# The opening of a gated attention and gated FFN kernel: x of the first segment in four tiles, wq by row halves

## The chip, the cores and the metric

The kernel runs on one core of a Trainium2 chip. The metric is device time in microseconds of one execution, as the median of several runs.

## The reference

One input x of 2048 tokens by 512 goes through two branches, and a gate per token mixes them. All tensors are bfloat16.

```python
g = sigmoid((x * gate_w).sum(-1, keepdims=True))
a = _A_ref(x, wq, wk, wv, wo, beta)      # 32 heads of 16, 4 segments of 512 tokens
b = (relu(x @ W_gate) * (x @ W_up)) @ W_down   # F = 1792
out = g * a + (1 - g) * b
```

In `_A_ref` each segment has causal softmax attention of its own (`a_dot`). From the second segment on a memory of the earlier segments is read too: `num = phi(q) @ M`, `den = phi(q) @ z + 1e-6`, with phi(t) = t + 1 for t > 0 and exp(t) otherwise. The two are mixed by a gate per head, sigmoid(beta), and projected by wo. After each segment M and z take in `phi(k)` and v.

## The kernel before

The work is written as some 1350 tasks, each for one engine, with a cost, a priority and what it depends on. Their order is not found when the kernel is built: it is written out by hand as a list of numbers, `ORDER`, and `UNITS` says which of the eight PSUM banks or ring buffers each task takes. So each engine works through a fixed queue. The figures in `LANDS` are the landing times of the first loads that the order was planned with; they make no instruction.

The token axis is cut into four segments of 512 tokens. For each segment TensorE makes q, k and v. The scores of four heads at a time are made in row mode: four matmuls side by side, each on 32 rows of the array. A score group (`score`, `qk`) fills four PSUM banks, ScalarE takes the exp of all four at once, GpSimd masks the diagonal pieces, and TensorE multiplies by v in column mode. Four such fills (`NFILL`) serve one unit of eight heads, and fill f takes heads of parity r = f % 2. Matmuls of the FFN and of the projections fill the time between. A full 128-wide matmul can also be issued as four of 32 columns side by side (lines L476 and L480 are the two forms), which the kernel does where TensorE is in column mode already.

The opening is what the change is about. SP's queue and ACT's queue each issue one DMA of x (`load_x0`, L267: two token tiles of 128 tokens each, the first 256 features) and one chunk of wq (`load_wq`, 128 rows). SP then issues a transposing DMA for the other half of the features (L304), the other two wq chunks, wk, wv and the FFN's weights. Meanwhile TensorE runs seven warm-up matmuls on a constant (`heat`, L922). Then `x0_tasks` turns the x tiles by matmuls with an identity matrix (L513), two token tiles into one bank, and DVE and ACT copy 256 columns at a time into `xT` (L528). ACT's first copy is preceded by its table load. One matmul on zeros, `junk` (L522), stands behind the flips.

`proj_q` of segment 0 takes the four wq chunks one by one, chunk 0 for all four heads' groups first; its results go to `QT` (DVE, L567). `proj_k` writes `ktr` (DVE, L583) and then three tasks write `KT` (L586): the even-parity half by `mcol_e`, the odd half by `mcol_o`, and a piece that only the diagonal groups read. A fill waits for `QT` and all three:

```python
e = score(key, lambda r=r, k=k: qk(u, r, k), [prj["q", seg, c]] + prj["k", seg, c], ...
```

Of the kernel before, what the change touches and what calls it, by code (L numbers as in the profile page):

```python
# [12 lines left out]
P = 128  # L13
# [8 lines left out]
NC = D // P  # L22
# [71 lines left out]
"""  # L94

UNITS = (
    "456701237654305000122212611232212100100000100000000130110000003000300002301130200031220202"
    "14113320353207112630381119110d320b102a221c100102102200031022000121112200033220200104563012"
    "000003200000002201100000320002000020011312212203031113a32230207013430163028200b21350219122"
    "c303d0112011031320210001131302032220322331021456721030000023000000022011000002300020000310"  # L100
    "111220213112163223212b3012121530243008013a01390037612d201c00121201322100312122323022013100"
    "145631200000023000000023011000000000000007001131230220103122362025300b320220081234211a0239"
    "715d4027326c10011200110"
)


class Slot:


    def __init__(self, cands):  # L110
        self.cands, self.units, self.left = tuple(cands), (), 0

    @property
# [66 lines left out]
def kernel(  # L180
# [74 lines left out]
    def work():  # L255
        return plan.one("ps", range(7, -1, -1))


    LANDS = dict(n0=3470, n1=3600, q0=4500, q1=4550, x0=5600, q2=5900, q3=6400, ka=7700,
                 kb=9600, v=11000, g0=12500, u0=13800, gw=14800, be=15100, g1=16300, u1=17500,  # L260
                 n2=18500, x1=21500, g2=22800, u2=23900, g3=25000, u3=26100)

# [726 lines left out]
```

## Time and profile before

| what | us |
| --- | --- |
| median of three runs (263.3 to 263.73) | 263.61 |
| the profiled execution | 263.58 |
| its span on the core | 261.9 |
| TensorE (PE) busy | 254.7 |
| VectorE (DVE) busy | 203.7 |
| ScalarE (ACT) busy | 183.2 |

The span is the time from the first to the last instruction of the core; about 1.7 us of the execution's time lie around it. A line of a timeline gives the start and the busy time of a group of instructions in us, the engine (PEld is the weight load, SPq and ACTq are DMA issues), the line of the kernel, the operation, what is written from what, and how often. In brackets stands how long the engine had been idle and what ended that.

### The profile page before, as it was taken

Reading aid. Unit: us, or ns where it says so; the run is one execution under the profiler, and the core shown is the slowest. Engines: PE = TensorE matmul, PEld = TensorE weight load, DVE = VectorE, ACT = ScalarE, POOL = GpSimd, SP = SyncE. Lnnn points to the kernel's source line nnn. Section 1 sums busy time; section 2 is a strip of 40 time slices with the busy share of each in tenths; the row PEclk is TensorE's granted clock in tenths of the full one; section 3 lists DMA queues with packets and bytes.
Section 4 is the critical chain, followed back from the end, with each engine's and each line's share of the span. In section 5 each row is a group of like instructions: output and inputs, shape, how many; then the busy total and the mean of one; then the engine's idle time right before and its main releaser. Section 6 shows DMA issues by size and latency. Waiting matters only on the chain.

```text
span 261.9 us, 8759 instructions
## 1 busy us (share of the span) xinstructions
PE 254.7 (97%) x3769; PEld 116.9 (45%) x3798; DVE 203.7 (78%) x472; ACT 183.2 (70%) x168; POOL 64.2 (25%) x168
## 2 busy tenths in 40 slices
PE   8899999999999999999999999999999999999995
PEld 3344434453444354544444444445444444445454
DVE  1899999888896756958989868858988678788622
ACT  2199998998877788787768576878486768972100
POOL 8023462313321223222112222122122232120000
PEclk9999999999999999999999999999999999999999
DMA  7999887021411202100210500140200100330011
GB/s 193 293 292 269 221 241 145 4 43 23 84 34 43 92 22 72 45 0 3 83 21 3 95 4 21 55 150 3 80 4 20 32 7 23 97 108 3 3 43 40
DMA packets 31581, 19.71 MB, mean 75 GB/s; under 512 B 16056, under 2 KB 30008, under 8 KB 31544
## 3 DMA queue, kind: packets, MB, share of 16 engines
q1 hardware_dynamic: 31128, 18.90, 27.1%
q8 instruction: 29, 0.48, 0.7%
q10 hardware_dynamic: 416, 0.26, 0.3%
q14 instruction: 8, 0.07, 0.1%
HBM read 13.21 MB, written 2.55 MB: 60 GB/s over the span
## 4 chain that ended last, share of the span: by engine, by line
PE 90%; DVE 5%; issue 1%; DMA 1%; SPq 1%; ACT 0%; DVEq 0%; ACTq 0%
PE ps L476 54%; PE ps L480 19%; PE ps L634 8%; PE ps L707 7%; DMA wq_sb<-in_A_wq_dram 1%; DVE ktr L583 1%; PE ps L647 1%; DVE KT L586 1%; PE ps L827 1%; SPq L304 1%; DVE QT L567 0%; PE ps L763 0%; DVE T L738 0%; DVE hT L877 0%; PE ps L803 0%
## 5 line engine op out<-in xcount | busy, mean ns | idle before, releaser
L656 ACT ACTIVATE E<-ps 128x2048 bf16<-128x2048 f32 x64 | 120.1, 1877 | 32.7 <-PE ps L634 22.5
L685 POOL TENSOR_SCALAR_AFFINE_SELECT E<-E 128x256 bf16<-128x256 bf16 x128 | 55.5, 458 | 170.3 <-ACT E L656 170.3
L877 DVE TENSOR_TENSOR hT<-ps,rgr 128x512 bf16<-128x512 f32 x56 | 37.8, 683 | 13.1 <-PE ps L476 8.4
L476 PE MATMUL ps<-xT,wu_sb 128*128 128x512 bf16 x163 | 45.6, 380 | 0.7 <-issue 0.5
L871 ACT ACTIVATE rgr<-ps 128x512 bf16<-128x512 f32 x56 | 32.6, 596 | 15.3 <-PE ps L480 8.2
L476 PE MATMUL ps<-wd_sb,hT 128*128 128x512 bf16 (+1 forms) x174 | 41.7, 354 | 0.6 <-issue 0.5
L476 PE MATMUL ps<-xT,wg_sb 128*128 128x512 bf16 x149 | 40.9, 380 | 0.3
L738 DVE STREAM_TRANSPOSE T<-ps 128x512 f32<-128x512 f32 x32 | 22.2, 705 | 6.7 <-PE ps L707 6.6
L634 PE MATMUL ps<-QT,KT 32*128 32x320 bf16 (+3 forms) x512 | 25.4, 273 | 0.3
L476 PEld LDWEIGHTS <-wu_sb 128*128 128x128 bf16 x170 | 15.3, 98 | 19.4 <-issue 3.0
L476 PEld LDWEIGHTS <-hT 128*128 128x128 bf16 x178 | 15.6, 98 | 17.6 <-issue 2.1
L903 DVE TENSOR_SCALAR osr<-ps,ngcol 128x512 bf16<-128x512 f32 (+2 forms) x18 | 12.3, 691 | 13.3 <-PE ps L480 9.1
L476 PEld LDWEIGHTS <-wg_sb 128*128 128x128 bf16 x156 | 14.3, 98 | 17.8 <-issue 2.1
L707 PE MATMUL ps<-E,Vp 128*17 128x320 bf16 (+3 forms) x512 | 19.4, 273 | 0.0
L634 PEld LDWEIGHTS <-KT 32*128 32x128 bf16 x512 | 7.6, 92 | 25.7 <-issue 24.6
L656 ACT ACTIVATE Em<-ps 128x2048 bf16<-128x2048 f32 x8 | 15.0, 1874 | 5.0 <-PE ps L647 5.0
L480 PE MATMUL ps<-xT,wg_sb 128*32 128x512 bf16 x272 | 17.8, 379 | 0.0
L476 PE MATMUL ps<-wv_sb,xT 128*128 128x512 bf16 x59 | 16.7, 380 | 0.8 <-DMA wv_sb<-in_A_wv_dram 0.6
L480 PE MATMUL ps<-wd_sb,hT 128*32 128x512 bf16 (+1 forms) x296 | 16.9, 359 | 0.0
L476 PE MATMUL ps<-xT,wq_sb 128*128 128x512 bf16 x57 | 15.8, 380 | 0.4 <-ACT xT L528 0.2
L476 PE MATMUL ps<-xT,wk_sb 128*128 128x512 bf16 x54 | 15.3, 379 | 0.2 <-issue 0.2
L480 PE MATMUL ps<-xT,wu_sb 128*32 128x512 bf16 x216 | 15.0, 379 | 0.0
(100 smaller groups left out, 293.1 us busy)
## 6 DMA issues: line engine op xcount, KB each, us to landing
out_dram<-osr SPq DMA_DIRECT2D x15, 128.0 KB
wd_sb<-in_B_W_down_dram SPq DMA_DIRECT2D x2, 896.0 KB
xn<-in_A_x_dram SPq DMA_DIRECT2D x3, 512.0 KB
cdr<-coefs SPq DMA_DIRECT2D x6, 256.0 KB
xn<-coefs SPq DMA_DIRECT2D x6, 256.0 KB
wg_sb<-in_B_W_gate_dram SPq DMA_DIRECT2D x2, 512.0 KB
wu_sb<-in_B_W_up_dram SPq DMA_DIRECT2D x2, 512.0 KB
wg_sb<-in_B_W_gate_dram SPq DMA_DIRECT2D x2, 384.0 KB
```

The source lines that it names most:

```text
L304: nc.sync.dma_start_transpose(out=xT[0][:, NC // 2:NC, :], in_=x[0:L, halves[1]])
L476: nc.tensor.matmul(out, lhsT=lhsT, rhs=rhs, start=start, stop=stop)
L480: nc.tensor.matmul(out[r], lhsT=lhsT[:, r], rhs=rhs, start=start, stop=stop, tile_position=(0, 32 * j))
L583: d = plan.add("DVE", 600, key - RQK, lambda: nc.vector.tensor_copy(ktr[ks.i][:], bank(sl)), [a], DVL + 40, need=[ks], frees=[sl])
L634: nc.tensor.matmul(ps[:, j * L + o:j * L + o + L - q], lhsT=KT[i][rows, kb, 3 * r:3 * r + 2].rearrange("p h q -> p (h q)"), rhs=QT[i][rows ...
L656: last_exp[0] = [plan.add("ACT", 66 + 4 * L / 1.2, key, lambda: nc.scalar.activation(dst, ps[:, 0:4 * L], ACT.Exp, scale=SCALE), [a] + war ...
L685: nc.gpsimd.affine_select(out=m[:, :, o:o + HP], in_=m[:, :, o:o + HP], compare_op=ALU.is_ge, fill=0.0, base=HP, pattern=[[0, 4], [1, HP]] ...
L707: nc.tensor.matmul(bank(sl)[32 * m:32 * m + HW, q:q + w], lhsT=(Vp[i] if n < 4 else Vm)[:, kb, r, 4 * c + j, 0:HW], rhs=rhs, start=(n == 0 ...
L738: done.append(plan.add("DVE", 633, key - RL, lambda r=r, sl=sl: nc.vector.transpose(T[ts.i][:, r], bank(sl)), [a] + done, 75 if r else 0, ...
L871: r = plan.add("ACT", 478, key - RL, lambda sl=gsl, rs=rs: nc.scalar.activation(rgr[rs.i][:], bank(sl), ACT.Relu), [g], ACL, frees=[gsl])
L877: nc.vector.tensor_tensor(hT[hs1.i][:], bank(sl), rgr[rs.i][:], ALU.mult)),
L903: nc.vector.tensor_scalar(osr[os.i][:, n0 - c0:n1 - c0], bank(sl)[:, 0:n1 - n0], ngcol[:, tt:tt + 1], None, ALU.mult)),
```

## The change

The first half of x of segment 0 is loaded by four DMAs of one token tile each, two on each queue. Chunks 0 and 1 of wq are each loaded by two DMAs of 64 rows, one on each queue. So each queue issues four DMAs instead of two before it goes on. Each token tile is turned by a matmul of its own, the four tiles of both feature chunks share four banks, and each tile is copied alone, 128 columns at a time, tiles 0 and 2 by DVE, 1 and 3 by ACT. The warm-up has five matmuls of 512 columns instead of six of 512 and one of 128. A fill waits for `QT` and only the half of `KT` with its own parity. `LANDS`, `ORDER` and `UNITS` are new throughout. In the new order the first fill of segment 0 stands before the first wv matmul, where before it stood behind six of them.

```diff
-    LANDS = dict(n0=3470, n1=3600, q0=4500, q1=4550, x0=5600, q2=5900, q3=6400, ka=7700,
...
+    LANDS = dict(n0=2950, n1=3000, n2=3200, n3=3250, q0=3950, q1=4350, x0=5600, q2=6000, q3=6700,
...
-    got_n[0] = [load_x0(eng, 2 * t, 2 * t + 2, halves[0], "n%d" % t)
-                for t, eng in enumerate((nc.sync, nc.scalar))]
+    queues = nc.sync, nc.scalar
+    got_n[0] = [load_x0(queues[t % 2], t, t + 1, halves[0], "n%d" % t) for t in range(4)]
...
-    got_q = [load_wq(nc.sync, 0), load_wq(nc.scalar, 1)]
+    got_q = []
+    for ci in range(2):
+        for rows, eng in ((slice(0, 64), nc.sync), (slice(64, P), nc.scalar)):
+            eng.dma_start(out=wq_sb[rows, ci, :], in_=A_wq[ci * P:(ci + 1) * P, :][rows, :])
+        got_q.append(arrival("q%d" % ci))
...
     def x0_tasks():
-        got, prev = [], None
+        got, prev = [[], []], None
+        slots = [work() for _ in range(4)]
         for ci in range(NC // 2):
-            for t in range(2):
-                sl = work()
...
+            for t, sl in enumerate(slots):
+                cols = slice(ci * P, (ci + 1) * P)
+                a = plan.add("PE", 107, K(-9 + ci) + t, lambda t=t, cols=cols, sl=sl: nc.tensor.matmul(
+                    bank(sl)[:, cols], lhsT=xn[:, t, cols], rhs=ident[:], start=True, stop=True),
+                    [got_n[0][t]], PEL, need=[] if ci else [sl], size=2)
...
+                got[ci].append(plan.add(
+                    "ACT" if t % 2 else "DVE", 225, K(-9 + ci) + t, lambda t=t, ci=ci, cols=cols, sl=sl: (
+                        nc.scalar.copy if t % 2 else nc.vector.tensor_copy)(
+                        xT[0][:, ci, t * P:(t + 1) * P], bank(sl)[:, cols]),
+                    [a], DVL, frees=[sl]))
...
-            e = score(key, lambda r=r, k=k: qk(u, r, k), [prj["q", seg, c]] + prj["k", seg, c],
+            e = score(key, lambda r=r, k=k: qk(u, r, k), [prj["q", seg, c], prj["k", seg, c][r]],
...
-        for k in range(7):
-            w = L if k < 6 else P
-            nc.tensor.matmul(bank(warm[k])[:, 0:w], lhsT=one.to_broadcast([P, P]),
-                             rhs=one.to_broadcast([P, w]), start=True, stop=True)
-    plan.add("PE", 3470, -1e9, heat, lat=0, need=warm, frees=warm, size=14)
+        for k in range(5):
+            nc.tensor.matmul(bank(warm[k]), lhsT=one.to_broadcast([P, P]),
+                             rhs=one.to_broadcast([P, L]), start=True, stop=True)
+    plan.add("PE", 2980, -1e9, heat, lat=0, need=warm, frees=warm, size=14)
```

More of the change, by code (lines that the diff above doesn't have):

```diff
@@ L30 @@
 ORDER = """
[63 rows of a table removed]
[63 rows of a table added]
 """
 UNITS = (
[L97 to L103, printed above, removed]
+    "456701237643212000032222111150123032300000230000000020110000011000000003201110201001222211"
+    "24111300151137222620280209221d213a102b002c001112000110010111203012222030133013301134563102"
+    "000003200000002201100000310001000020011222201203031022b22132227303431062018013a10353109103"
+    "c012d0112021031222132011221322032300332323011145613020000022000000032011000000100020000020"
+    "117021223020241233000a2122112811363215023b31392237023d002c10010112103110002111322225112031"
+    "2456231000000220000000330110000022000000072011322a3121203020342232211311062117321530082219"
+    "015c623b104d12000110021"
 )
@@ L256, in work @@
         return plan.one("ps", range(7, -1, -1))
-    LANDS = dict(n0=3470, n1=3600, q0=4500, q1=4550, x0=5600, q2=5900, q3=6400, ka=7700,
-                 kb=9600, v=11000, g0=12500, u0=13800, gw=14800, be=15100, g1=16300, u1=17500,
-                 n2=18500, x1=21500, g2=22800, u2=23900, g3=25000, u3=26100)
+    LANDS = dict(n0=2950, n1=3000, n2=3200, n3=3250, q0=3950, q1=4350, x0=5600, q2=6000, q3=6700,
+                 ka=7500, kb=9000, v=11100, g0=12500, u0=13500, gw=14400, be=14700, g1=16000,
+                 u1=17200, n4=18300, x1=21500, g2=22800, u2=23900, g3=25000, u3=26100)
     def arrival(name):
@@ L314 @@
     load_gu(1)
-    got_n[0].append(load_x0(nc.sync, 0, NC, halves[1], "n2"))
+    got_n[0].append(load_x0(nc.sync, 0, NC, halves[1], "n4"))
     load_xT(1)
@@ L505, in x0_tasks @@
     def x0_tasks():
-        got, prev = [], None
+        got, prev = [[], []], None
+        slots = [work() for _ in range(4)]
         for ci in range(NC // 2):
-            for t in range(2):
-                sl = work()
-                def flip(t=t, ci=ci, sl=sl):
-                    for k in range(2):
-                        nc.tensor.matmul(bank(sl)[:, k * P:(k + 1) * P],
-                                         lhsT=xn[:, 2 * t + k, ci * P:(ci + 1) * P], rhs=ident[:],
-                                         start=True, stop=True)
-                a = plan.add("PE", 214, K(-9 + ci) + t, flip, [got_n[0][t]], PEL, need=[sl], size=4)
+            for t, sl in enumerate(slots):
[3 more added lines that the diff above has]
+                    [got_n[0][t]], PEL, need=[] if ci else [sl], size=2)
                 if prev:
@@ L519, in x0_tasks @@
                 prev = a
-                if ci == 1 and t:
-                    js = work()
-                    j = plan.add("PE", 214, K(-9 + ci) + t, lambda js=js: nc.tensor.matmul(
-                        bank(js)[:, 0:2 * P], lhsT=junk[:, 0:P],
-                        rhs=junk[:, None, 0:P].to_broadcast([P, 2, P]), start=True, stop=True),
-                        [a], lat=0, need=[js], frees=[js], size=2)
-                b = plan.add(
-                    "ACT" if t else "DVE", 80 + (0.95 if t else 1.12) * P * 2,
-                    K(-9 + ci), lambda t=t, ci=ci, sl=sl: (
-                        nc.scalar.copy if t else nc.vector.tensor_copy)(
-                        xT[0][:, ci, 2 * t * P:2 * (t + 1) * P], bank(sl)[:, 0:2 * P]),
-                    [a], DVL, frees=[sl])
-                got.append(b)
-        x0_first.extend([got[0:2] + [(j, 0.0)], got[2:4]])
-        return [got, [got_x0b]]
+                got[ci].append(plan.add(
[3 more added lines that the diff above has]
+                    [a], DVL, frees=[sl]))
+        js = work()
+        j = plan.add("PE", 214, K(-8) - 1, lambda: nc.tensor.matmul(
+            bank(js)[:, 0:2 * P], lhsT=junk[:, 0:P],
+            rhs=junk[:, None, 0:P].to_broadcast([P, 2, P]), start=True, stop=True),
+            [prev], lat=0, need=[js], frees=[js], size=2)
+        x0_first.extend([got[0] + [(j, 0.0)], got[1]])
+        return [got[0] + got[1], [got_x0b]]
     def proj_mm(w, c, seg):
```

126 rows, old and new, of the table ORDER are left out of this document.

## The prediction

> **What bounds the kernel now.** I read the page's busy shares first, then who waited for whom, then the timeline of the first 16 us.
>
> ```profile
> span 261.9 us, 8759 instructions
> PE 254.7 (97%) x3769; PEld 116.9 (45%) x3798; DVE 203.7 (78%) x472; ACT 183.2 (70%) x168; POOL 64.2 (25%) x168
> PE   8899999999999999999999999999999999999995
> PE 90%; DVE 5%; issue 1%; DMA 1%; SPq 1%; ACT 0%; DVEq 0%; ACTq 0%
> PEld L476 <- DMA wv_sb<-in_A_wv_dram: 1.1, 1, 1.1
> PEld L476 <- DMA wq_sb<-in_A_wq_dram: 0.9, 2, 0.5
> ```
>
> TensorE is busy in every slice, and it carries the chain. There are 3798 weight loads but only 3769 matmul records. The holes of 0.22 us that the timeline shows after 12 us are as long as one matmul, and there are about as many as lost records, so I read them as lost records. The only real waits of TensorE are for DMAs of wq and wv, and they lie before 11.6 us. From 11.51 us TensorE runs without a break to its last matmul, which ends at 259.0; 2.9 us of eviction and output DMA follow. So the change can pay only by what happens before 11.51, or cost by opening a hole later.
>
> ```profile
> 0.80 0.48 ACTq L267 DMA_DIRECT2D xn<-in_A_x_dram  x1
> 0.84 2.82 PE L922 MATMUL ps<-const-bfloat16-1.0 128*128 128x512 bf16 x7 [0.84 <-PEq L973]
> 1.31 0.53 ACTq L267 DMA_DIRECT2D wq_sb<-in_A_wq_dram  x1
> 1.83 1.31 SPq L304 DMA_TRANSPOSE xT<-in_A_x_dram  x1
> 1.87 1.28 ACT L528 ACT_TABLE_LOAD   x1 [1.87 <-issue]
> 3.19 1.05 SPq L267 DMA_DIRECT2D wq_sb<-in_A_wq_dram  x2
> 3.46 0.75 PE L513 MATMUL ps<-ident,xn 128*128 128x128 bf16 x8
> 4.03 0.65 ACT L528 CAST xT<-ps 128x256 bf16<-128x256 f32 x2 [0.88 <-PE ps L513]
> 4.49 3.84 PE L476 MATMUL ps<-xT,wq_sb 128*128 128x512 bf16 x16 [0.16 <-ACT xT L528]
> 6.43 1.41 PEld L476 LDWEIGHTS <-wq_sb 128*128 128x128 bf16 x8 [0.55 <-DMA wq_sb<-in_A_wq_dram]
> 7.50 2.48 DVE L567 CAST QT<-ps 128x512 bf16<-128x512 f32 x4 [2.83 <-PE ps L476]
> 10.09 1.29 DVE L583 CAST ktr<-ps 128x512 bf16<-128x512 f32 x2
> 11.51 0.98 PEld L476 LDWEIGHTS <-xT 128*128 128x128 bf16 x6 [1.08 <-DMA wv_sb<-in_A_wv_dram]
> 12.91 0.40 PE L634 MATMUL ps<-QT,KT 32*128 32x448 bf16 x8
> 13.24 0.55 PEld L476 LDWEIGHTS <-wg_sb 128*128 128x128 bf16 x4 [0.21 <-issue]
> ```
>
> These rows give the opening. Warm-up matmuls go first, then eight flips, copies on DVE and ACT, and eight wq matmuls of chunks 0 and 1 from 4.49. TensorE stands about 0.22 us for chunk 2 of wq, until 6.43. Then come eight more wq and twelve wk matmuls, to 10.76, and a stand of 0.75 us until wv is there at 11.51. The first score fill (QT, KT) comes after six wv matmuls.
>
> **The work that stays.** In the instruction order of the two programs the matmuls of 512 columns are 682 whole and 912 quarter-width ones before, 656 and 1016 after. Four quarters run side by side, so that is 910 full ones in both. The turns between full, row, column and quad mode are 151 in both. What TensorE does from the first wq matmul on is therefore the same, and the new order costs nothing by itself, covered by equal work. To see whether it opens holes later I compared the distance from one score group to the next with ScalarE's work between its exps (1.88 us each, 0.6 us for a relu). The tightest place lacks 0.77 us before and 0.39 us after, and the lists are alike through most of the first two segments. Before, no hole came of it. The shorter wait of the later fills for their K half is worth nothing there, since TensorE never stands for KT after 11.51.
>
> **The opening, step by step.** *Warm-up:* two matmuls less, one of 512 and one of 128 columns, at 0.427 and 0.107 us (the starts in the trace). The flips could begin at 2.93 instead of 3.46. *Flips:* the same eight matmuls, waiting for four tiles. The bytes of x are the same and start at the same time, so the last tile lands about when the two DMAs of before do (3.3 and 3.5 by the semaphore records). That gains little, and it is not what decides:
>
> *ACT's copies.* Before, two DMA issues stand ahead of ACT's table load; after, four do. At 0.51 and 0.56 us each (starts 0.80, 1.31, 1.87) the load starts at 2.94 and ends at 4.22. Two copies of chunk 0 follow. The 256-column copy takes 0.37 us, 0.27 from start to start; relu at 512 columns takes 0.59, so 0.88 ns per column, and a 128-column copy is an estimated 0.26 us, 0.16 from start to start. They end at 4.64, TensorE sees them 0.09 later, and wq starts at 4.73, so 0.24 us later than before. If issues of smaller DMAs were as short as 0.43 us (the shortest of SP's row), it is 4.4. The eight matmuls of 0.216 us end at 6.46.
>
> The Trainium skill, "ScalarE: Activation LUTs", section "What ACT_TABLE_LOAD costs", adds 1.38 us of drain to a load of 1.28 us, 2.66 us in all. By that figure wq would start at 6.11 and the run be some 1.1 us longer. The trace speaks against it: the first copy started 2.16 us after the load's start.
>
> *Chunk 2 of wq.* SP issues two DMAs more ahead of the transposing load, so that load and all behind it are issued 1.02 us later (2 x 0.51). The bounds for the landing are no shift (TensorE goes on at 6.46, when chunk 1 is done) and the whole 1.02 (7.45). The packet records say that the DMA engines were busy with x and wq until 4.0, so the transposing load waited in line anyway. A later transposing load, with nothing ahead of it, moves its first packets 1.2 us after its issue, here 4.1 instead of 3.5. Chunk 2, issued at 4.22, can then start 1.1 us later (as the first x DMA: 0.81 to 1.93) at 5.34, 0.56 later than before. But its landing before was late by 0.44 for one of its sixteen parts alone. I take half of 0.56, nearer to the small bound, and go on at 6.68.
>
> *wk and the first fill.* In the new order the fill stands before wv and needs only its own half of KT. From 6.68 (call it t0): the first chunk-3 matmul ends after 4 x 0.216 + 0.38, DVE sees it 0.04 later, four QT copies take 0.60 each from start to start, ktr 0.69, the wait for it 0.08, one KT half 0.34 (instead of three), and TensorE follows 0.09 later. That is t0 + 4.89. TensorE's own 20 matmuls are through at t0 + 4.31, so it stands 0.58 us for KT. The fill is at 11.57, and wv follows 0.33 later (12.91 to 13.24 in the rows) at 11.90.
>
> *wv.* By the semaphore records it landed at 11.47, one part 0.46 later than the rest. Shifted like chunk 2 (half of 0.56; bounds 0 and 1.02) that is 11.75, hidden behind the fill. The next load, wg, landed at 12.90, is then due by 13.22 and is wanted at 11.90 + 6 x 0.216 = 13.19: 0.03 at most.
>
> *Sum.* Before, wv began at 11.51 with the fill still to do: 0.33, and 0.10 for the turn into row mode (0.31 instead of 0.216 between starts), level with 11.94. After: 11.90 plus 0.03. The same in stands of TensorE counted from 4.49: before 0.22 and 0.77, in all 0.99; after 0.24 (later wq), 0.22 (chunk 2), 0.58 (KT) and 0.03 (wg), in all 1.07, less the 0.10 of the turn into row mode, which now falls into the stand for KT: -0.02, so 0.0 us. On the profiled execution's 263.58 (span 261.9 and 1.7 around it) that gives 263.6; it lies 0.03 under the median of 263.61. Its own range: no DMA shift gives 11.69, -0.25; a shift of 0.56 for all gives 12.2, +0.25.
>
> **Rivals.** (1) *SP's two issues pass through whole.* Chunk 2 at 7.45, wv at 12.67, wg just in time: +0.74, 264.3. For it: everything behind the transposing load is in one queue. Against: the DMA engines had a backlog when that load was issued. It decides where the backlog ends before 4.1 us. (2) *The clock comes late.* The matmul starts show 0.427 us per 512 columns until 3.68 and 0.216 afterwards, after 2.83 us of unbroken work. Now the warm-up stops at 2.93, tiles may be awaited, and up to 0.9 us of standing follow the flips. If the count began anew at 4.73, matmuls would be slow until 7.56: 6.6 done, the other 1.4 end at 7.86, wv at 13.1, +1.15, 264.7. Against: most of that gap lies after 3.68. The Trainium skill, "TensorE: Matmul & The Clock Gate", part 1, has a free-running window of 3.4 us that must be busy; by it the next grant would come at 7.09 and cost 0.9 us. No run shows yet how much standing is forgiven. (3) *Faster.* ACT's issues are short and chunk 2 lands whole at 5.95, as fifteen of its sixteen parts did: wq starts at 4.4, t0 = 6.13, the fill comes at 11.02, and wv at 11.51 as before, or at 11.35 if its straggler goes too: -0.43 to -0.59, 263.05. (4) *A hole later.* One or two of the tight places in the new order open by 0.4 us: 264.2. (5) The drain rule above: 264.7.
>
> **How the numbers follow.** Forecast 0.50, rivals 0.17, 0.08, 0.15, 0.09, 0.01. About 0.2% (0.5 us) is what a measurement of this kernel can tell from no change. Faster than that are the better two thirds of rival 3 and a little of the forecast, where stragglers fall better still: 0.14. Slower is 1, 2, 5 and most of 4: 0.32. The rest is 0.54. The range from 262.95 to 264.4 holds the forecast's own (263.3 to 263.85), rivals 1 and 4 and most of 3; it leaves out rivals 2 and 5.
>
> **What would show it.** The table load at 2.9 and wq at 4.7; TensorE waiting for wq around 6.7; a stand before the first fill that ends on DVE's KT, at 11.5; no wait for wv; no hole after 14 us. I am wrong if wq starts at 4.2, if chunk 2 is awaited past 7.2, if matmuls at 5 us take 0.43, or if TensorE stands later than 17 us.

## The result: slower by 0.7%

| | us |
| --- | --- |
| changed kernel, median of 6 runs (265.43 to 266.42) | 265.52 |
| kernel before in the same comparison, median of 6 (263.3 to 264.31) | 263.97 |
| ratio, with its 95% interval | 1.0072 [1.0050, 1.0094] |
| profiled execution of the changed kernel; its span | 266.4; 264.5 |

The forecast was 263.6, the range ended at 264.4, and slower had 0.32. The profiled execution lies 0.9 us above its median, so the profile below overstates the loss somewhat. The ratio is the mean over the six pairs of runs, so it is not the quotient of the two medians (1.0059).

From the page of the changed kernel, and from the list of what the weight load waited for:

```profile
span 264.5 us, 8906 instructions
PE 254.9 (96%) x3844; PEld 117.1 (44%) x3874; DVE 206.3 (78%) x474; ACT 183.7 (69%) x170; POOL 63.0 (24%) x168
PE   8789999999999999999999999999999999999995
PE 86%; DMA 4%; SPq 3%; DVE 2%; issue 2%; ACT 1%; DVEq 0%; ACTq 0%
PEld L480 <- DMA wq_sb<-in_A_wq_dram: 2.0, 2, 1.4
PEld L480 <- DMA wg_sb<-in_B_W_gate_dram: 1.7, 2, 1.2
```

TensorE's busy time is what it was (254.9 against 254.7); the span grew by 2.6. In the chain, DMA and SP's issues went from 1% each to 4% and 3%, and TensorE's second and third slices (6.6 to 19.8 us) show 7 and 8 tenths where they showed 8 and 9. So the time is lost in the opening, waiting for loads. The timeline of the changed kernel says where:

```profile
0.81 0.87 SPq L267 DMA_DIRECT2D xn<-in_A_x_dram  x2
1.73 1.45 SPq L306 DMA_DIRECT2D wq_sb<-in_A_wq_dram  x2
2.94 1.28 ACT L522 ACT_TABLE_LOAD   x1 [2.94 <-issue]
3.22 1.34 SPq L308 DMA_TRANSPOSE xT<-in_A_x_dram  x1
4.24 0.77 ACT L522 CAST xT<-ps 128x128 bf16<-128x128 f32 x4
4.75 1.89 PE L480 MATMUL ps<-xT,wq_sb 128*128 128x512 bf16 x8 [0.23 <-ACT xT L522]
7.59 1.19 PEld L480 LDWEIGHTS <-wq_sb 128*128 128x128 bf16 x7 [1.45 <-DMA wq_sb<-in_A_wq_dram]
12.41 0.40 PE L632 MATMUL ps<-QT,KT 32*128 32x448 bf16 x8 [0.28 <-DVE KT L584]
13.36 1.46 PE L480 MATMUL ps<-wv_sb,xT 128*128 128x512 bf16 x5 [0.55 <-DMA wv_sb<-in_A_wv_dram]
14.76 0.11 PEld L480 LDWEIGHTS <-wg_sb 128*128 128x128 bf16 x2 [0.44 <-DMA wg_sb<-in_B_W_gate_dram]
19.15 0.11 PEld L480 LDWEIGHTS <-wg_sb 128*128 128x128 bf16 x2 [1.25 <-DMA wg_sb<-in_B_W_gate_dram]
```

TensorE starts on wq at 4.75, almost as early as forecast, and then stands five times for a load: 1.12 us for chunk 2 of wq (6.48 to 7.60), 0.04 for wk, 0.62 for wv, 0.11 for wg and 0.92 for wg's second piece (18.23 to 19.15). A stand is counted here from start to start of two matmuls, less the 0.216 us that one takes (for wv, less the 0.33 that the fill ahead of it took). After 19.2 it does not stand for a load again. Its last matmul ends at 261.47, 2.47 later than before.

What held up the loads stands in the fourth row. The transposing load was issued at 1.83 before; now it is issued at 3.22. Everything behind it in SP's queue moved with it, as the landing records show (us):

| landed | before | changed | later by |
| --- | --- | --- | --- |
| transposing load of x | 5.53 | 6.76 | 1.23 |
| chunk 2 of wq | 6.39 | 7.55 | 1.17 |
| wk, second half | 8.40 | 9.78 | 1.38 |
| wv | 11.47 | 13.32 | 1.85 |
| wg, second piece | 16.33 | 19.11 | 2.78 |

A load lands in sixteen parts, and it counts as landed with the last. Of wv and of wg's second piece the last part came 0.94 and 1.26 us after the other fifteen in this execution (0.46 and 0.04 before); those fifteen were later by 1.37 and 1.56 only. So the two long stands at 13 and 19 us are in part chance. `after_ht` below has the same loads and was profiled at 265.38, close to the median: there chunk 2 was awaited 1.08 us, but wv 0.03 and wg's second piece 0.23.

### The profile page after: what moved, and what is told of

It is laid out like the page before. It is cut to its first block, busy times and chain, and to the rows that moved or that the text cites. A ratio compares the mean times of both kernels' runs of the same rounds, so it can differ in the third digit from the quotient of the medians.

```text
span 264.5 us, 8906 instructions
## 1 busy us (share of the span) xinstructions
PE 254.9 (96%) x3844; PEld 117.1 (44%) x3874; DVE 206.3 (78%) x474; ACT 183.7 (69%) x170; POOL 63.0 (24%) x168
## 4 chain that ended last, share of the span: by engine, by line
PE 86%; DMA 4%; SPq 3%; DVE 2%; issue 2%; ACT 1%; DVEq 0%; ACTq 0%
PE ps L480 48%; PE ps L484 21%; PE ps L632 7%; PE ps L705 7%; DMA xn<-in_A_x_dram 4%; SPq L267 2%; DVE junk L434 1%; PE ps L645 1%; ACT E L654 1%; PE ps L825 1%; SPq L308 1%; PE ps L761 0%; PE ps L801 0%; SPq L316 0%; SPq L314 0%
## 5 line engine op out<-in xcount | busy, mean ns | idle before, releaser
L683 POOL TENSOR_SCALAR_AFFINE_SELECT E<-E 128x256 bf16<-128x256 bf16 x128 | 54.3, 448 | 174.8 <-ACT E L654 174.6
L480 PE MATMUL ps<-xT,wu_sb 128*128 128x512 bf16 x176 | 47.9, 380 | 0.7 <-issue 0.5
L480 PE MATMUL ps<-xT,wg_sb 128*128 128x512 bf16 x153 | 42.6, 380 | 1.1 <-DMA wg_sb<-in_B_W_gate_dram 0.8
L480 PE MATMUL ps<-wd_sb,hT 128*128 128x512 bf16 (+1 forms) x143 | 32.9, 348 | 0.5 <-issue 0.5
L480 PEld LDWEIGHTS <-wu_sb 128*128 128x128 bf16 x184 | 16.8, 98 | 21.2 <-issue 3.0
L484 PE MATMUL ps<-wd_sb,hT 128*32 128x512 bf16 (+1 forms) x416 | 24.4, 365 | 0.0
L480 PEld LDWEIGHTS <-hT 128*128 128x128 bf16 x148 | 12.6, 98 | 14.3 <-issue 2.3
L480 PE MATMUL ps<-wv_sb,xT 128*128 128x512 bf16 x56 | 15.9, 380 | 0.9 <-DMA wv_sb<-in_A_wv_dram 0.5
L480 PE MATMUL ps<-xT,wq_sb 128*128 128x512 bf16 x52 | 14.9, 380 | 1.4 <-DMA wq_sb<-in_A_wq_dram 1.0
L565 DVE CAST QT<-ps 128x512 bf16<-128x512 f32 x16 | 10.8, 688 | 5.9 <-PE ps L480 5.8
```

The lines of the kernel that those rows point to most:

```text
L480: nc.tensor.matmul(out, lhsT=lhsT, rhs=rhs, start=start, stop=stop)
L484: nc.tensor.matmul(out[r], lhsT=lhsT[:, r], rhs=rhs, start=start, stop=stop, tile_position=(0, 32 * j))
L565: prj["q", seg, c] = plan.add("DVE", 600, key - RQK, lambda: nc.vector.tensor_copy(QT[i][:], bank(sl)), [a], DVL, frees=[sl])
L683: nc.gpsimd.affine_select(out=m[:, :, o:o + HP], in_=m[:, :, o:o + HP], compare_op=ALU.is_ge, fill=0.0, base=HP, pattern=[[0, 4], [1, HP]] ...
```

## The experiments

Theory A: the four extra DMAs hold up SP's queue, and all loads behind them are late. Theory B: the new opening itself costs, by the shorter warm-up (a late clock), the eight small copies, or a hole that the new order opens later. All ratios are to the kernel before on the same chip, five rounds each, with 95% intervals. "Issued" and "landed" are those of the transposing load in the profile. Single profiles vary: in five kernels that issue it at 1.83 it landed between 5.53 and 6.01.

| kernel | issued | landed | wv landed | ratio |
| --- | --- | --- | --- | --- |
| before | 1.83 | 5.53 | 11.47 | 1 |
| *order of before* | | | | |
| before_warm5 | 1.83 | 5.92 | 11.20 | 0.9994 [0.9984, 1.0004] |
| act_q0 | 1.33 | 7.43 | 10.93 | 1.0020 [1.0008, 1.0032] |
| x4_only | 2.20 | 5.55 | 12.08 | 1.0020 [1.0007, 1.0033] |
| cols_only | 2.29 | 6.16 | 11.24 | 1.0007 [0.9997, 1.0017] |
| late_T | 2.77 | 7.20 | 11.57 | 1.0025 [1.0013, 1.0036] |
| halves_only | 2.81 | 6.39 | 12.22 | 1.0028 [1.0015, 1.0042] |
| dma_only | 3.23 | 6.69 | 12.18 | 1.0045 [1.0030, 1.0061] |
| *new order* | | | | |
| rest_act_q0 | 1.32 | 7.15 | 10.65 | 1.0045 [1.0032, 1.0059] |
| rest7_ht | 1.83 | 6.01 | 10.75 | 1.0005 [0.9995, 1.0014] |
| rest_warm7 | 1.83 | 5.91 | 11.08 | 1.0025 [1.0015, 1.0035] |
| rest_only | 1.83 | 5.84 | 11.39 | 1.0034 [1.0013, 1.0056] |
| wq_whole | 2.20 | 6.01 | 11.68 | 1.0021 [1.0007, 1.0036] |
| pairs_fixed | 2.30 | 6.22 | 12.14 | 1.0026 [1.0017, 1.0036] |
| x_pairs | 2.83 | 6.26 | 11.22 | 1.0049 [1.0028, 1.0069] |
| after_cols | 2.98 | 6.26 | 12.14 | 1.0058 [1.0042, 1.0075] |
| after_fixed | 3.01 | 6.12 | 11.97 | 1.0053 [1.0036, 1.0069] |
| after_ht | 3.21 | 6.54 | 12.65 | 1.0062 [1.0044, 1.0080] |
| changed kernel | 3.22 | 6.76 | 13.32 | 1.0072 [1.0050, 1.0094] |
| after_warm7 | 3.32 | 6.65 | 11.88 | 1.0056 [1.0036, 1.0075] |

### The loads alone and the rest alone

`dma_only` is the kernel before with the new loads of x and wq, its own order, copies and warm-up:

```diff
+    for t in range(4):
+        (nc.sync, nc.scalar)[t % 2].dma_start(
+            out=xn[:, t:t + 1, halves[0]],
+            in_=x[t * P:(t + 1) * P, halves[0]].rearrange("(t p) n -> p t n", p=P))
...
+        for rows, eng in ((slice(0, 64), nc.sync), (slice(64, P), nc.scalar)):
+            eng.dma_start(out=wq_sb[rows, ci, :], in_=A_wq[ci * P:(ci + 1) * P, :][rows, :])
```

> The kernel before with nothing changed but its first loads: x of segment 0 by four DMAs, chunks 0 and 1 of wq by two DMAs of 64 rows each. Order, flips, copies, warm-up and the fills' waits are those of before. Theory A (the load queue: four more DMAs ahead of the transposing load push it from 1.83 to about 3.2 us, half by SP's two extra issues, half because the ninth DMA reuses the semaphore of the first and waits for its landing): the transposing load is issued at 3.2, chunk 2 of wq is seen at 7.6 instead of 6.4, wv lands at 13 instead of 11.5, and the run is 1.4 to 2.8 us slower than before. Theory B (the new order, the flips or the late clock cost the time): within 0.3 us of before.

`rest_only` is the other half: the changed kernel with x in two DMAs and wq whole, as before.

```diff
-    got_n[0] = [load_x0(queues[t % 2], t, t + 1, halves[0], "n%d" % t) for t in range(4)]
+    for t in range(2):
+        queues[t].dma_start(out=xn[:, 2 * t:2 * t + 2, halves[0]], in_=x[
+            2 * t * P:(2 * t + 2) * P, halves[0]].rearrange("(t p) n -> p t n", p=P))
...
+    got_q = [load_wq(nc.sync, 0), load_wq(nc.scalar, 1)]
```

> The changed kernel with the first loads of before (x in two DMAs, wq chunks whole), all else as changed. Theory A: transposing load at 1.83 again, chunk 2 at 6.4, first fill at 11.3, wv at 11.65 with the fill done; 0.1 to 0.4 us faster than before or no change. Theory B: still 1.4 us or more slower than before, with the clock late (matmuls of 0.43 us after 4.5 us) or with holes after 14 us.

Measured: 265.44 (+0.45%) and 265.09 (+0.34%, runs from 263.85 to 266.42). Both theories have something: the loads cost about 1.2 us with the old order, and the rest costs with the old loads too. The two add up to the whole (0.72%), but that is partly a coincidence: what the rest costs here hardly occurs in the changed kernel's profile, as shown below. `dma_only` lost a little less than the 1.4 us of theory A. `rest_only` fits neither theory: no loss was expected by the one, 1.4 or more by the other, and it lost about 0.9. Where the changed kernel loses more than `dma_only` no run shows; the two intervals overlap.

### Which of the loads

`x_pairs` and `wq_whole` take one of the two edits of the loads out of the changed kernel: x in two DMAs again, or wq whole again, by the lines of the diff above.

> The changed kernel with x of segment 0 in two DMAs as before; the wq halves stay. Only six DMAs stand ahead, so the transposing load reuses no semaphore. Theory A, split: it is issued after three issues of SP at about 2.4; if the wait for the semaphore is the main part, wv lands within 0.6 us of before and the run is within 0.5 us of before; if each issue passes through whole, it is about 0.7 us slower. Theory B: as slow as the changed kernel.

> The changed kernel with chunks 0 and 1 of wq whole, one on each queue, as before; the four x tiles stay. Theory A, split: transposing load at about 2.2 without a wait, wv within 0.6 us of before, run within 0.5 us of before. If small DMAs themselves cost (many issues at once), this and x_pairs differ. Theory B: as slow as the changed kernel.

Measured +0.49% without the four tiles of x, more than theory A allowed, and +0.21% without the halves of wq, about as it had it. The halves cost more than the tiles, although both add as many issues. The issue rows show a difference. In `x_pairs` and the changed kernel two issues of a half (64 rows) take 1.45 us on SP's queue, the first 0.57 and the second 0.83 by the issue records; a whole chunk ahead of the transposing load takes 0.42 to 0.46 there. That led to two more kernels: `halves_only` is the kernel before with the row halves alone, and `cols_only` has column halves in their place, 128 rows of 512 bytes.

```diff
-        for rows, eng in ((slice(0, 64), nc.sync), (slice(64, P), nc.scalar)):
-            eng.dma_start(out=wq_sb[rows, ci, :], in_=A_wq[ci * P:(ci + 1) * P, :][rows, :])
+        for c, eng in ((slice(0, D // 2), nc.sync), (slice(D // 2, D), nc.scalar)):
+            eng.dma_start(out=wq_sb[:, ci, c], in_=A_wq[ci * P:(ci + 1) * P, c])
```

> The kernel before with chunks 0 and 1 of wq loaded by row halves on the two queues, and nothing else changed. Load theory: the halves, not the tiles of x, are what delays the transposing load: it is issued at about 2.8 us instead of 1.83 and lands at 6.2 to 6.4, chunk 2 of wq at 7.1 to 7.4, wv 0.5 to 1.0 later than in the kernel before; 0.7 to 1.3 us slower. Rival: the number of DMAs ahead of it counts, and two more of them are half of what the four cost; 0.3 to 0.6 us slower.

> The kernel before with chunks 0 and 1 of wq loaded by column halves (128 rows of 512 B) on the two queues instead of row halves. If the issue of DMAs over half the rows is what is slow (.57 and then .83 to .88 us), these are issued in .45 to .50 each, the transposing load goes at 2.3 to 2.35 us, and the kernel is 0 to 0.6 us slower than before. If any half of a chunk issued by both queues at once costs the same, the transposing load goes at 2.7 to 2.8 and the time is that of the row halves.

SP's issue rows of `halves_only`:

```profile
1.32 1.45 SPq L306 DMA_DIRECT2D wq_sb<-in_A_wq_dram  x2
2.81 1.33 SPq L308 DMA_TRANSPOSE xT<-in_A_x_dram  x1
```

and of `cols_only`, with the row of the wait that followed:

```profile
1.32 0.93 SPq L306 DMA_DIRECT2D wq_sb<-in_A_wq_dram  x2
2.29 1.33 SPq L308 DMA_TRANSPOSE xT<-in_A_x_dram  x1
7.21 1.41 PEld L480 LDWEIGHTS <-wq_sb 128*128 128x128 bf16 x8 [1.26 <-DMA wq_sb<-in_A_wq_dram]
```

Equal bytes and equally many DMAs; the row halves are issued in 1.45 us and cost 0.28%, the column halves in 0.93 and cost 0.07%, which is not told from nothing. So it is the row halves that are dear, and their slow issue is what the rows show: in `halves_only` the transposing load and the next ones up to wv are issued 0.5 us later than in `cols_only`, and wv lands at 12.22 against 11.24. Whether the issue alone is the cause is not shown, for the row halves also left the DMA engines emptier (busy 0.64 from 3 to 4 us and 0.80 from 4 to 5 us, against 0.95 and 1.10). The last row teaches something else: TensorE stood 0.93 us for chunk 2 and nothing was lost, because it then found wv there (no stand at 11.5, where the kernel before had stood 0.75). In this chain of loads the early wait cost only what it added to the last one. Why the second issue of a half takes twice as long as a whole chunk, no run says.

`x4_only`, the kernel before with x in four tiles and nothing else:

> The kernel before with x's first half loaded as four DMAs of one token tile instead of two of two, and nothing else. Load theory: the transposing load goes .40 us later (2.23 instead of 1.83), chunk 2 of wq and wv come some .4 later; with TensorE's stand at wv of .25 to .75 us in the kernel before, 0 to 0.5 us slower (+0.1 to +0.2%). Rival: no cost, the loads make it up: within 0.1%.

+0.20%: the transposing load went at 2.20, but landed no later than in the kernel before's profile (5.55); wv landed 0.6 later.

### The warm-up

`before_warm5` is the kernel before with five warm-up matmuls; `rest_warm7` and `after_warm7` are `rest_only` and the changed kernel with the seven of before.

```diff
-        for k in range(7):
-            w = L if k < 6 else P
-            nc.tensor.matmul(bank(warm[k])[:, 0:w], lhsT=one.to_broadcast([P, P]),
-                             rhs=one.to_broadcast([P, w]), start=True, stop=True)
+        for k in range(5):
+            nc.tensor.matmul(bank(warm[k]), lhsT=one.to_broadcast([P, P]),
+                             rhs=one.to_broadcast([P, L]), start=True, stop=True)
```

> The kernel before with a warm-up of five matmuls instead of seven and nothing else changed. Clock theory: the full clock comes late in some executions (granted 7 to 10 us instead of 3.8), each wq matmul before it takes .427 instead of .216, and the median is 0.3 to 1.2 us higher with a wider spread than that of the kernel before. Rival: the gap between warm-up and flips is short enough here, and no change above 0.3 us is seen.

> The kernel before's loads (x in two pairs, wq whole), the change's new order of turns, copies and fills, and the kernel before's warm-up of seven matmuls instead of five. Clock theory: what the version with five lost (+0.34% in the median, spread 263.85 to 266.42, twelve wq matmuls at .427 us) is the short warm-up and the idle gap after it; with seven the full clock is granted before or soon after wq starts, the median falls to 263.5 to 264.0 and the spread to under 1 us. Rival: the new order itself (copies on ScalarE behind the table load, four flips, fills on their own half of KT) costs; then it stays near 265.0 with the clock granted as early as in the kernel before.

> The changed kernel with the kernel before's warm-up of seven matmuls. If the shorter warm-up's late clock is hidden behind the wait for chunk 2 of wq (which ends at 7.6 us whatever the first eight matmuls take), there is no gain: 265.2 to 265.8 us, as the changed kernel. Rival: the clock costs the changed kernel something after all; then 264.7 to 265.1.

Measured -0.06%, +0.25% and +0.56%. The clock theory fails in the kernel before: a shorter warm-up costs nothing there. In the two other places seven matmuls are better by 0.09 and 0.16 of a per cent, inside the intervals. The clock does come late at times, and not by the length of the warm-up alone: the first wq matmul at full speed came at 4.56 (`cols_only`), 4.71 (`act_q0`) and 6.7 us (`halves_only`, `dma_only`) with seven matmuls, and at 4.75 (changed kernel), 5.05 (`before_warm5`), 7.3, 8.7 and 10.0 (`wq_whole`, `x_pairs`, `rest_only`) with five. In most of these the slow matmuls only fill time in which TensorE would have waited for chunk 2. The wide spread of `rest_only`, whose chunk 2 came early, fits a price there; the comparison with `rest_warm7` does not settle it.

### The hole behind VectorE

`rest_warm7` has the loads and the warm-up of before, and still costs 0.25%. A place after the loads where TensorE can be held up lies at 25 us of its timeline:

```profile
23.34 0.69 DVE L433 SCALAR_TENSOR_TENSOR junk<-xn,gwb 128x512 bf16<-128x512 bf16 x1
24.38 1.27 DVE L874 TENSOR_TENSOR hT<-ps,rgr 128x512 bf16<-128x512 f32 x2
24.57 0.11 PEld L479 LDWEIGHTS <-xT 128*128 128x128 bf16 x2
24.57 0.39 PE L479 MATMUL ps<-wv_sb,xT 128*128 128x512 bf16 x1
25.10 0.81 PE L479 MATMUL ps<-xT,wg_sb 128*128 128x512 bf16 x3
```

The wg matmul at 25.10 starts when the first of the two products hT ends (25.05) and frees its bank. The expectation below counts 0.31 us for this hole. But two weights of xT were loaded, and only one wv matmul is on record: the second, from 24.79 on, is a lost record. From 24.57 to 25.10 is 0.53 us, where the same three matmuls take 0.44 in `rest7_ht` (25.00 to 25.44). So the hole is 0.09 us in this execution. It is larger in the profiles of four other kernels of the new order: 0.34 in `wq_whole`, 0.33 in `x_pairs`, 0.32 in `rest_act_q0` and 0.33 in `rest_only`, where wg follows a wv matmul that started at 27.08:

```profile
27.62 1.24 PE L479 MATMUL ps<-xT,wg_sb 128*128 128x512 bf16 x5 [0.17 <-DVE hT L874]
```

The products stand in VectorE's queue behind the last two of segment 0's gate sums (L433) and a piece of KT. `rest7_ht` moves one of these sums, and the load that follows it, behind the products (task 59 is the sum, 361 the load, 246 the second product):

```diff
-    240 245 81 56 59 361 109 692
+    240 245 81 56 109 692
...
-    258 150 431 246 151
+    258 150 431 246 59 361 151
```

> The version with the loads and the warm-up of the kernel before and the change's new order, with one edit in that order: VectorE's fourth multiply-and-add of the gate sums (and the next segment's load of x that follows it) is put behind two products hT instead of ahead of them. In the profile of that version TensorE stood .31 us at 24.6 us, waiting for the first of these products to free a bank of PSUM (0.5 us in a sister version). If this hole is a part of what the new order costs, it is gone and the time is 0.2 to 0.4 us below that version's (264.38, +0.25% on the kernel before): +0.1 to +0.17%. Rival: the hole is given back later or opens elsewhere, and the ratio stays at +0.2 to +0.3%.

In its timeline wg follows wv without a gap, and the sum comes after:

```profile
25.00 0.60 PE L476 MATMUL ps<-wv_sb,xT 128*128 128x512 bf16 x2
25.44 0.81 PE L476 MATMUL ps<-xT,wg_sb 128*128 128x512 bf16 x3
25.53 0.68 DVE L430 SCALAR_TENSOR_TENSOR junk<-xn,gwb 128x512 bf16<-128x512 bf16 x1
```

+0.05% in place of +0.25%, and the two intervals do not overlap: with this one move the new order, eight small copies and early fill included, equals the old when the loads are early. It brings no gain. The move gives back about 0.5 us; the hole that the profiles show accounts for 0.09 to 0.34 of it, and what the rest is stays open.

### The transposing load earlier, or later

`act_q0` puts chunk 0 of wq on ACT's queue too, so that SP issues the transposing load right behind x; `rest_act_q0` does the same in `rest_warm7`. `late_T` delays that load in the kernel before by two loads of beta that nothing reads.

```diff
-    got_q = [load_wq(nc.sync, 0), load_wq(nc.scalar, 1)]
+    got_q = [load_wq(nc.scalar, 0), load_wq(nc.scalar, 1)]
```

```diff
+    for k in range(2):
+        nc.sync.dma_start(out=sb([P, H], BF16, "late%d" % k)[:], in_=A_beta.partition_broadcast(P))
     nc.sync.dma_start_transpose(out=xT[0][:, NC // 2:NC, :], in_=x[0:L, halves[1]])
```

> The kernel before with chunk 0 of wq issued on ScalarE's queue instead of SyncE's, so that the transposing load is issued at about 1.32 us instead of 1.83. Load theory: what is issued ahead of the transposing load sets when it and all behind it land; it lands .4 to .5 us earlier (5.0 to 5.1 instead of 5.53), chunk 2 of wq at 5.6 to 6.0, wv some .5 earlier, and the time falls by 0.2 to 0.7 us. Rival: the landings are set by bytes in flight, not by the place in the queue: they stay within .15 us, and so does the time.

> The change's new order with x in pairs, a warm-up of seven, and chunks 0 and 1 of wq both whole on ScalarE's queue, so that SyncE issues the transposing load right behind one pair of x (about 1.3 us). If both theories hold (early loads and an early clock are what pays), 0.3 to 0.8 us faster than the kernel before. If only the queue counts and the order costs, between -0.3 and +0.5 us. Against it: ScalarE issues one more DMA ahead of its table load, so the first copy and wq start some .4 to .6 us later, at about 5.3 to 5.6 us.

> The kernel before with two loads of beta (8 KB each, into tiles that nothing reads) on SyncE's queue ahead of the transposing load; wq and x as before. Theory: what costs is when the transposing load is issued, and all behind it with it; two issues of about .45 put it at 2.7 to 2.8 us instead of 1.83, and the time rises as in the version with row halves (load at 2.81): +0.25 to +0.4%. Rival: the price is in the halves themselves (smaller DMAs on two queues), not in the delay; within 0.1% of the kernel before.

The first two missed (+0.20% and +0.45%, where none of their outcomes was that slow). From `act_q0`:

```profile
1.33 1.31 SPq L304 DMA_TRANSPOSE xT<-in_A_x_dram  x1
7.23 2.27 PEld L476 LDWEIGHTS <-wq_sb 128*128 128x128 bf16 x12 [1.97 <-DMA wq_sb<-in_A_wq_dram]
```

Issued 0.5 earlier, the load landed 1.9 later than in the kernel before (7.43), and chunk 1 of wq, sharing the DMA engines with that load's 256-byte packets, only at 7.19. From 4 to 6 us the core's DMAs moved 141 and 164 GB/s, where the kernel before moved 267 and 224. So the place in the queue is not all: issued this early, the load was on its way together with the chunks that are wanted first. `late_T` costs 0.25% without any halves or tiles, as expected. It is not the delay alone, though: its two small loads landed only at 6.0 and 6.2, and the transposing load at 7.20, 4.4 us after its issue, where the other versions in this order, `act_q0` aside, show 3.3 to 4.1.

### The repairs in the changed kernel

`after_cols` has column halves in the changed kernel, `after_ht` the moved gate sum, `after_fixed` both and the warm-up of seven; `pairs_fixed` is `after_fixed` with x in two DMAs.

> The changed kernel with chunks 0 and 1 of wq by column halves (128 rows of 512 B) instead of row halves. Theory: the issue of the row halves (.57 + .83 us) delays all loads behind them; with .45 each the transposing load goes at 2.65 to 2.75 instead of 3.22, chunk 2 of wq comes at 6.9 to 7.2, and the kernel is 0.5 to 0.9 us faster than the changed one: +0.35 to +0.55% on the kernel before. Rival: in this order what counts is the number of DMAs ahead, not their issue; it stays at +0.6 to +0.8%.

> The changed kernel with VectorE's fourth gate sum behind two products hT. In the changed kernel's profile TensorE didn't stand at 24 to 26 us, because it had already stood .9 us for wg at 18 us. If the hole is hidden there by the later loads, no gain: +0.6 to +0.8% on the kernel before. Rival: the order's share (0.2%) is independent of the loads; then +0.45 to +0.55%.

> The changed kernel with column halves of wq, the gate sum behind the two products, and the warm-up of seven. If the loads' issue and the hole are the whole of the loss, it comes back to the kernel before within 0.1%: 263.8 to 264.3 us. If x in four tiles costs for itself, +0.15 to +0.3%. If the new start (first copies, first fill on half of KT) gains anything, below the kernel before by up to 0.3 us.

> The version with column halves of wq, the gate sum behind the two products and the warm-up of seven (265.0 us, +0.53%), with x in two DMAs again instead of four. Six DMAs are then ahead of the transposing load instead of eight, and it needs no DMA's end. Theory: it is issued at 2.3 us instead of 3.0, lands at 6.0 to 6.2 instead of 6.5, and the time falls to that of the column halves alone plus the order without its hole: +0.05 to +0.2% (263.9 to 264.3). Rival: the loss is in the new order together with any halves; it stays at +0.4 to +0.55%.

Measured +0.58%, +0.62%, +0.53% and +0.26%. The first three lie within the changed kernel's interval; `after_cols` lies between its two outcomes, and `after_fixed` met none of its three. That the moved sum brings nothing there fits the first theory: in the changed kernel's profile the wg matmul behind the two wv (27.40) is 0.01 us late, in `after_cols` 0.06, in `after_warm7` 0.12. Why the hole is this small there was not tested. That column halves bring so little has a reason of its own, in SP's rows of `after_cols`:

```profile
1.73 0.90 SPq L306 DMA_DIRECT2D wq_sb<-in_A_wq_dram  x2
2.98 1.31 SPq L308 DMA_TRANSPOSE xT<-in_A_x_dram  x1
```

SP is through with the halves at 2.63 but issues the transposing load at 2.98. The landing records use eight semaphores in turn, and with four tiles and four halves this load is the ninth DMA: it takes over the semaphore of one of the first x tiles, which landed at 2.968. In `after_fixed` that tile landed at 2.992 and the load went at 3.01; in `after_warm7`, 3.307 and 3.32; in the changed kernel itself, 3.187 and 3.22. So two causes ended at the same time in the changed kernel: the slow issue of the row halves (to 3.18) and the wait for a tile of x (to 3.19). Taking one away left the other, and the load went at 2.83 with the row halves alone (`x_pairs`) and at 2.98 with the wait alone. Only with x in two DMAs is the load issued at 2.30, and then half of the loss is gone (+0.53 to +0.26%). The remaining 0.26% is above the 0.05 to 0.2% expected, and more than `cols_only` and `rest7_ht` together (0.12%): in this order TensorE again stood for wk, wv and wg (0.34, 0.36, 0.38), whose loads came as late as with worse versions (wv at 12.14). Why the same loads landed 0.9 later than in `cols_only` stays open. No version beats the kernel before by more than its interval.

## Why the prediction was wrong

*ACT's copies and the start of wq: right, by some luck.* The table load started at 2.94, the copies at 4.24 and wq at 4.75 (forecast 4.73). The four issues ahead of the table load took 2.13 us together, as forecast, but each was off: the x tiles took 0.44 and 0.49, the row halves 0.57 and 0.63 from start to start, where 0.51 and 0.56 were taken for both. The drain of the Trainium skill, "ScalarE: Activation LUTs", section "What ACT_TABLE_LOAD costs", is not there in this trace either: the first copy starts 0.02 us after the load's end.

*Chunk 2 of wq: the step that failed.* It took half of 0.56 for the shift of the landing, between bounds of 0 and 1.02; it was 1.17, outside both. Two terms of it were wrong. The first is the issue: 2 x 0.51 came from whole DMAs, and the row halves took 0.57 and 0.83, so the load was issued 1.39 later and not 1.02. The wait for a tile of x, for which the forecast had no term, would have held it as long. The second is the backlog, which was to absorb half of the delay: the transposing load's first packets were to move at 4.1, 0.6 later than before, and half of that to reach chunk 2. By the packet records they moved at 4.63 instead of 3.63, 1.00 later, and the load landed 1.23 later. Fifteen of the sixteen parts of chunk 2 then came 1.60 later (7.55 instead of 5.95); it was 1.17 in all only because the late last part of before, which the forecast rightly saw as chance, did not recur. With the new loads there was less backlog. Busy share of the DMA engines and GB/s are the last two columns of these rows by the microsecond, first of the kernel before, then of the changed one:

```profile
3.00:4.00 1.00, 1.00 (x11) 0.72 (x10) 0.08 (x1) 0.15 (x1) 1.00 (x1) 1.00 1.07 325
4.00:5.00 1.00, 0.84 (x8) 0.40 (x6) 0.67 (x2) 0.65 (x2) 0.99 (x6) 1.00 1.21 267
```

```profile
3.00:4.00 1.00, 1.00 (x9) 0.71 (x8) 0.00 (x0) 1.00 (x1) 1.00 (x1) 1.00 0.63 177
4.00:5.00 1.00, 0.77 (x6) 0.31 (x5) 0.90 (x4) 0.99 (x5) 0.98 (x6) 1.00 0.62 160
```

While the row halves were under way (to 5.34), the DMA engines were little more than half busy, and what they did not move between 3 and 5 us (592 - 337 GB/s over a microsecond, some 255 KB) came later. The landing followed the issue at nearly the same distance (3.70 before, 3.54 after; 3.1 to 4.4 in the other kernels that issue it at 1.83 or later).

*wk and the first fill: right from there on.* t0 + 4.89 with t0 = 7.60 is 12.49; the fill came at 12.41. The stand for KT was 0.44 instead of 0.58.

*wv and wg: the same error, grown.* wv was to be shifted by 0.28 and hidden; it came 1.85 later and was waited for. The sum had no term for wg's second piece, which cost 0.92 us in this profile; it was issued at 10.21 instead of 8.39. Here the late sixteenth parts add to the error. The forecast's sum, term by term (us of stand):

| stand of TensorE | forecast | measured |
| --- | --- | --- |
| later start of wq | 0.24 | 0.26 |
| chunk 2 of wq | 0.22 | 1.12 |
| wk | 0 | 0.04 |
| KT, turn into row mode included | 0.58 | 0.44 |
| wv | 0 | 0.62 |
| wg, first piece | 0.03 | 0.11 |
| wg, second piece | no term | 0.92 |
| in all, less 0.10 for the turn and 0.99 of before | 0.0 | 2.42 |

The last matmul ended 2.47 later, so these terms are nearly the whole of what this profile lost.

*The rivals.* Rival 1, SP's delay passing through whole, was the right mechanism, with 0.17 and a price too small (0.74 us, from the same 1.02). Rival 4, a hole later, exists (up to 0.34 us behind the products hT), but hardly in the changed kernel's profile (0.01). Rival 2 did not occur in the changed kernel's profile: every wq matmul from 4.75 ran at 0.216 from start to start. That the new order costs nothing by itself was not right: with the loads and the warm-up of before it costs 0.25%, and 0.05% once one gate sum is moved. Two of the prediction's own signs of being wrong came: chunk 2 was awaited past 7.2, and TensorE stood later than 17 us.

## What to carry to other kernels

Before a DMA is split, look at what is queued behind it: the issue time of the added pieces is put on every load behind them, and the run pays as far as the last of these loads is waited for. Do not count on a backlog of the DMA engines to absorb the delay, for the split itself can shrink that backlog. When two causes hold the same instruction, an experiment that removes one may show nothing; look for what the instruction waits for next. And before a hole is read from start times, count the weight loads: a lost matmul record looks like a wait.

## What the runs showed of the hardware

- Issuing a DMA over 64 of the 128 rows on both queues at once took SP 0.57 to 0.58 us for the first and 0.82 to 0.85 for the second (six profiles); 128 rows of half the length took 0.42 to 0.46 each, and a whole chunk in the same place 0.42 to 0.46. The Trainium skill, "DMA: Bandwidth & Descriptors", section "Rules for kernel authors", advises against two transfers to disjoint halves of the partitions, because they share the same engines; these runs agree (+0.28% against +0.07% for column halves) and add that the issue takes longer too.
- A DMA that takes over a semaphore still in use is issued 0.01 to 0.04 us after the earlier DMA's landing (four profiles above).
- The granted clock became full at 3.5 us (`rest_act_q0`) to 10.0 us (`rest_only`) among kernels with nearly the same opening. The Trainium skill, "TensorE: Matmul & The Clock Gate", part 1, has a free-running window and a number of slow matmuls that varies from run to run; these profiles agree (0 to 12 slow wq matmuls), and no price of it could be told in the medians.
- A transposing DMA of 256-byte packets that was issued at 1.33 us, beside two wq chunks on the other queue, landed at 7.43 and the second chunk at 7.19 (`act_q0`). Issued at 1.83, with one chunk on each queue, the two landed at 5.53 and 4.56 (kernel before).
